# Dilated-window attention and a leaky-ReLU MLP in one kernel: joined value casts in the first two batches, two entries of the planner's cost list, and another order of the first loads

## The chip, the cores and the metric

The kernel runs on one core of one Trainium2 chip. The metric is the device time of one launch in microseconds (us). The kernel before has a median of 294.21 us over 3 runs (293.82 to 296.23).

## The reference

Eight batches of 8 heads with 576 tokens and 64 features go through causal window attention. Heads 0 to 3 look back over 32 neighbouring tokens, heads 4 to 7 over 128 tokens in steps of 4 ("dilated"). The result is laid out as 4608 tokens by 512 features and goes through two matrix products with a leaky ReLU between them.

```
mask_plain = (rel >= 0) & (rel < window)
mask_dil = (rel >= 0) & (rel < window * dilation) & (rel % dilation == 0)
masks = np.stack([mask_plain if h < H // 2 else mask_dil for h in range(H)], axis=0)
scores = np.where(masks[None, :, :, :], scores, -1000000000.0)
attn = np.exp(scores - np.max(scores, axis=-1, keepdims=True))
attn = attn / (np.sum(attn, axis=-1, keepdims=True) + 1e-09)
x = np.matmul(attn, v).transpose(0, 2, 1, 3).reshape(B * S, H * D)
h = x @ w_in
return np.maximum(0.01 * h, h) @ w_out
```

Here window is 32, dilation 4, w_in is 512 x 2048 and w_out 2048 x 512. Inputs and output are float32; the kernel computes with float16 operands.

## The kernel before, in words

**Pairs of heads.** Two heads share a tile of 128 partitions. The program calls such a pair `vi`: pairs 0 and 1 are plain, 2 and 3 dilated, and they are visited in the order 2, 3, 0, 1. For each pair a region of the tile `slots` holds the keys and queries (features on partitions) and the values (tokens on partitions), all in float16.

**Two ways of doing attention.** Batches 0 and 1 (`EARLY`, line 29) are done before the rest of the kernel is under way. q and k arrive as float32 tiles `stg`, are cast to `nat` (line 701 when ACT casts, line 702 otherwise), turned by TensorE (line 940) into PSUM, and moved from there to `slots` (line 713 on ACT, 714 on DVE). A unit (line 1027 on) is half a pair: scores (lines 1073 and 1076), the exponential on ACT (1083), the sums (1094), the values product (1088), logarithm and exponential of the sums on ACT (1104 and 1106), and the product with the reciprocal into `xt` on DVE (1117). The last 64 tokens of all pairs are one more unit, "rest" (lines 1154 to 1193). Batches 2 to 7 are done in bursts on quarters of the array (line 1278) between other work.

**Value casts.** `load_v` (from line 765) fetches v for four heads at a time into `vst`: group 1 (`g == 1`, dilated) first, group 0 after it. In batches 0 and 1 the dilated group is cast to `slots` in 12 pieces, six for each of the two pairs: four of 64 partitions x 256 elements and two of 64 x 64. A pair's values product waits for the pair's own six.

**The MLP.** Chunks of 384 tokens run through `up` (line 1407, 16 blocks of 128 hidden features; in the first chunk each of the four `vi` blocks is a task by itself) or, for the second chunk, `up_pair` (line 1441), ACT evicts with leaky ReLU (1423, 1454), and the second product follows (line 1620 for the first tiles, 1709 after). From chunk 8 on the first product is done with seven instead of eight products (line 1540).

**What sets the order.** Nothing is issued in the order of the Python code. Every operation is added to a plan with the engines that may do it, a cost for each, and a priority. A list scheduler goes forward and backward over the plan (line 543 on), takes the backward times as priorities, adds a number per task from the table `NUDGE` (line 42), and lets the table `HAND` (line 282) cut a task's choice of engines. Its last forward pass fixes engine and order of every instruction. Idle stretches of TensorE in the plan are filled with matmuls on a tile of zeros, `warm` (line 1983), which keep it active and give nothing to the output. The costs of a cast stand in `cast` (line 695), those of a move out of PSUM in `move` (line 712 on).

**The first loads.** The string `FIRST` (line 40) is the order of the loads of batches 0 and 1 and of the weights: `q01` is q and k of batch 0, group 1, `r0` the last 64 tokens' q and k of batch 0, `v01` its dilated values, `w0` to `w7` the eight blocks of w_in (512 KB each; `w0` to `w3` are the first 1024 hidden features for pairs 2, 3, 0, 1), `w8` to `w15` those of w_out, `c` a table of constants. All go to SP's queue but k of `q01` and the constants with the identity matrix, which go to ACT's. Group 0's first q goes into `stg2`, and so on in turn.

## Time and profile before

| | |
|---|---|
| median of 3 runs | 294.21 us |
| the three runs | 296.23, 294.21, 293.82 us |
| the profiled execution's own time | 294.69 us |
| its span (first to last instruction) | 292.9 us |
| mean granted TensorE clock in it | 0.992 |
| PE busy, share of the span | 283.5 us, 97% |
| DVE, ACT, POOL busy | 225.0, 214.4, 87.8 us |
| real work of PE, without the matmuls on zeros | begins at 6.90 us with line 940 |
| first matmul of the MLP | 23.06 us |

How to read it: the page has busy time per engine, then the span in 40 slices with the busy share in tenths, the clock that the throttle granted to TensorE and the DMA share, then the chain of work that ended last, then groups of instructions. A table by stage shows the same for stretches of one's choice. A timeline row has start, length, engine, line, what is written and read, how many instructions are merged in the row, and in brackets how long the engine sat idle before it and what ended that.

### The profile page before, as it was taken

To read this page: it belongs to the slowest core of one execution; us is meant where nothing else is said; L and a number is where in the kernel's file an instruction comes from. 1 tells how busy PE (TensorE), PEld (TensorE's weight loads), DVE (VectorE), ACT (ScalarE), POOL (GpSimd) and SP (SyncE) were. 2 spreads that over 40 slices of the span, in tenths; PEclk is the share of its full clock that TensorE was granted. 3 is DMA by queue.
4 is the path that set the end of the run, shared out by engine and by line. 5 is a ranking of instruction groups with operands and counts; after the bars stand their busy time and mean duration, and the time that the engine had idled before them with its cause. 6 is when DMAs were issued, how large, how long until landed. Compare 5 with 4: busy or idle time off the path is not lost.

```text
span 292.9 us, 9624 instructions
## 1 busy us (share of the span) xinstructions
PE 283.5 (97%) x3983; PEld 222.1 (76%) x3983; DVE 225.0 (77%) x445; ACT 214.4 (73%) x451; POOL 87.8 (30%) x149
## 2 busy tenths in 40 slices
PE   7879999999999999999999999999999999999995
PEld 3656877686676767776767777878899999999984
DVE  6695577855789469965967978999987879888773
ACT  3996898688988996899888778895556777745421
POOL 4334532371371734352742752630200000000000
PEclk9979999999999999999999999999999999999999
DMA  7999999895999988799999888411212010112123
GB/s 253 316 350 402 388 289 325 225 229 83 143 188 198 214 153 168 138 200 226 180 206 176 163 171 199 134 40 38 73 38 74 1 38 2 36 38 74 47 98 107
DMA packets 140043, 47.04 MB, mean 161 GB/s; under 512 B 118752, under 2 KB 137440, under 8 KB 140000
## 3 DMA queue, kind: packets, MB, share of 16 engines
q1 hardware_dynamic: 139312, 45.81, 62.9%
q8 instruction: 31, 0.51, 0.7%
q10 hardware_dynamic: 688, 0.63, 0.6%
q14 instruction: 12, 0.10, 0.1%
HBM read 36.99 MB, written 9.44 MB: 158 GB/s over the span
## 4 chain that ended last, share of the span: by engine, by line
PE 88%; ACT 4%; DVE 3%; DMA 2%; issue 1%; ACTq 0%; DVEq 0%
PE psum L1709 32%; PE psum L1407 24%; PE psum L1540 13%; PE psum L1278 6%; PE psum L1620 5%; PE psum L1441 3%; DMA con<-consts 2%; PE psum L940 1%; DVE slots L702 1%; ACT slots L713 1%; PE psum L1094 1%; PE psum L1088 1%; DVE xt L1117 1%; PE psum L1073 1%; DVE slots L714 1%
## 5 line engine op out<-in xcount | busy, mean ns | idle before, releaser
L1407 PE MATMUL psum<-xt,w_in 128*128 128x384 f16 x448 | 84.8, 326 | 0.1
L1709 PEld LDWEIGHTS <-gt 128*128 128x128 f16 x768 | 74.5, 98 | 11.7 <-issue 0.5
L1423 ACT ACTIVATE gt<-psum 128x384 f16<-128x384 f32 x112 | 53.3, 492 | 15.0 <-PE psum L1407 13.0
L1709 PE MATMUL psum<-w_out,gt 128*128 128x256 f16 x512 | 63.6, 273 | 0.3 <-DVE stg L1740 0.3
L1407 PEld LDWEIGHTS <-w_in 128*128 128x128 f16 x448 | 41.7, 98 | 23.5 <-issue 0.5
L702 POOL CAST nat<-stg 128x576 f16<-128x576 f32 (+1 forms) x50 | 33.5, 693 | 43.5 <-DVE gt L1695 21.3
L702 POOL CAST slots<-vst 64x256 f16<-64x256 f32 (+4 forms) x56 | 27.0, 496 | 24.9 <-DMA vst<-in_v_dram 13.9
L1360 DVE TENSOR_TENSOR xt<-psum,rc 128x448 f16<-128x448 f32 (+2 forms) x52 | 20.3, 429 | 15.9 <-ACT rc L1343 14.8
L1559 DVE TENSOR_TENSOR vst<-psum,vst 128x384 f32<-128x384 f32 x48 | 25.7, 552 | 5.7 <-PE psum L1540 2.7
L1563 ACT ACTIVATE gt<-vst 128x384 f16<-128x384 f32 (+1 forms) x32 | 21.7, 684 | 7.9 <-DVE vst L1559 7.8
L701 ACT CAST slots<-vst 64x256 f16<-64x256 f32 (+4 forms) x54 | 22.5, 429 | 1.0
L1377 ACT ACTIVATE ee<-psum 128x896 f16<-128x896 f32 (+3 forms) x30 | 21.4, 721 | 2.5 <-PE psum L1278 2.4
L1552 ACT COPY vst<-psum 128x384 f32<-128x384 f32 x29 | 13.6, 475 | 11.7 <-PE psum L1540 11.2
L1540 PEld LDWEIGHTS <-w_in 128*128 128x128 f16 x256 | 21.9, 98 | 0.3
L1540 PE MATMUL psum<-xt,w_in 128*128 128x192 f16 x192 | 20.9, 246 | 0.0
L714 DVE COPY slots<-psum 128x512 f16<-128x512 f16 (+3 forms) x22 | 10.3, 477 | 11.5 <-PE psum L940 4.3
L1384 DVE TENSOR_TENSOR ee<-ee,con 128x768 f16<-128x768 f16 (+1 forms) x24 | 14.4, 599 | 6.2 <-ACT ee L1377 6.1
L1746 DVE TENSOR_TENSOR osb<-psum,stg 128x512 f32<-128x512 f32 x21 | 14.3, 682 | 4.1 <-ACT stg L1738 2.3
L926 POOL COPY slots<-slots 128x512 f16<-128x512 f16 (+1 forms) x15 | 10.2, 690 | 23.7 <-DVE slots L919 17.2
L1540 PEld LDWEIGHTS <-stg 128*128 128x128 f16 x192 | 16.7, 98 | 0.5
L1738 ACT COPY stg<-psum 128x512 f32<-128x512 f32 (+1 forms) x18 | 9.9, 549 | 9.6 <-PE psum L1709 9.0
L1343 ACT ACTIVATE rc<-rc 128x576 f32<-128x576 f32 x24 | 16.6, 691 | 0.1
(107 smaller groups left out, 501.7 us busy)
## 6 DMA issues: line engine op xcount, KB each, us to landing
out_dram<-osb SPq DMA_DIRECT2D x32, 256.0 KB, 2.6
stg<-in_q_dram SPq DMA_DIRECT2D x40, 144.0 KB, 3.5
stg<-in_k_dram SPq DMA_DIRECT2D x40, 144.0 KB, 3.7
vst<-in_v_dram SPq DMA_DIRECT2D x16, 288.0 KB, 4.8
vst<-in_v_dram SPq DMA_DIRECT2D x8, 512.0 KB, 5.9
gt<-in_moe_w_in_dram SPq DMA_DIRECT2D x6, 512.0 KB, 7.4
stg<-in_q_dram SPq DMA_DIRECT2D x5, 512.0 KB, 5.6
stg<-in_k_dram SPq DMA_DIRECT2D x5, 512.0 KB, 6.5
```

What stands on the lines that cost most here:

```text
L701: return nc.scalar.copy(out=dst, in_=src)
L702: return ENG[e].tensor_copy(out=dst, in_=src)
L1278: jobs.append(lambda: nc.tensor.matmul(at(bk, q0, q1, x, *od), lhs(p0, p1, q), rhs(p0, p1), start=first, stop=last, skip_group_check=True, ...
L1343: lambda e: nc.scalar.activation(out=rt, in_=rt, func=AF.Exp, scale=-1.0), prio)
L1360: lambda e, args=args: nc.vector.tensor_tensor(out=args[0], in0=args[1], in1=args[2], op=ALU.mult), prio)
L1377: lambda e, p=p, np=np, part=part: nc.scalar.activation(out=at(et, 0, 128, 448 * p, [448, np], [1, n]), in_=part, func=AF.Exp, scale=SCALE ...
L1407: nc.tensor.matmul(ht[:, 0:n], at(w_in, 0, 128, vi * DFF + j // 2 * 256 + j % 2, [2, 128]), at(xt[m % 2], 0, 128, vi * 1152 + x0 + x, [1, n]),
L1423: lambda e: nc.scalar.activation(out=gt[c % NG][:, j * n_c + x:j * n_c + x + n], in_=ht[:, 0:n], func=AF.Prelu, alpha=0.01),
L1540: nc.tensor.matmul(bk[:, n * i:n * i + n], w(v, 2 * z + i), x(v), start=first and i == 0 and v == 0, stop=i == 1 and v == 1, skip_group_ch ...
L1559: return add("DVE", 0.08 + 2 * n * 0.00104, deps, lambda e: nc.vector.tensor_tensor(out=dst, in0=over(bk), in1=dst, op=ALU.add), begin + w ...
L1563: t = add("ACT", dur, deps + gt_free.get(c - NG, []), lambda e: nc.scalar.activation(out=dst, in_=src, func=AF.Prelu, alpha=0.01), begin + ...
L1709: nc.tensor.matmul(bk[:, x:x + HN], tl[:, off + j * step:off + j * step + 128], rhs(j), start=first and x == 0 and j == 0, stop=j == HJ - ...
```

## The change

It has five parts.

1. **Joined value casts.** In batches 0 and 1 the dilated group's casts take both pairs in one instruction: 64 x 2x4x64 and 64 x 2x64 in place of two of half the size. That makes 6 casts of 12 in each of the two batches. Both pairs' values products now wait for all six.
2. **Costs of casts.** DVE's listed cost gets a fixed part of 0.16 in place of 0.08, ACT's 0.20 in place of 0.085; the part per element stays.
3. **Cost of the dilated key moves.** Their listed cost per element on DVE goes from 0.00127 to 0.00052.
4. **The first loads.** `r0` comes before `q00`; `w3` comes before `w6`; some of the later ones change places.
5. **The tables.** `NUDGE` and `HAND` are replaced, `PLACE`, `PACE`, `SERVE` and the banks of the early turns (`TURN_AT`) are set a little differently.

Each PE matmul that computes something is there as often as before. Of those on zeros there are 3 more. Over the whole program DVE has 9 instructions more (456), ACT 13 fewer (443), POOL 8 fewer (146).

```diff
-SERVE = 1.1
+SERVE = 1.08
...
-PLACE = 20.5
-PACE = 4.6
+PLACE = 20.0
+PACE = 4.65
...
+OWN = 0.16
+JOIN = (0, 1)
...
-FIRST = ('q01 q00 r0 w7 v01 v00 w0 w1 w2 w6 w3 w4 q11 w5 w9 q10 v11 w10 '
-         'w8 w13 w11 r1 v10 w15 w12 w14 c ')
+FIRST = ('q01 r0 q00 w7 v01 v00 w0 w1 w2 w3 w6 w4 q11 w5 w9 q10 v11 w10 '
+         'w13 w8 w15 w11 r1 v10 w12 c w14 ')
 NUDGE = {
-    0: 87.72, 2: -74.14, 3: 109.34, 4: -121.33, 5: -62.38, 6: 44.63, 7: 83.91, 8: -101.47, 9: 29.63,
...
 HAND = {
-    3: "DVE", 4: "DVE", 5: "DVE", 6: "DVE", 8: "DVE", 11: "DVE", 12: "DVE", 13: "DVE", 26: "DVE",
...
+    9: "POOL", 26: "POOL DVE", 28: "ACT", 29: "POOL", 33: "DVE", 36: "DVE ACT", 45: "ACT", 48:
...
-TURN_AT = ('fgfgt', 't0tft')
+TURN_AT = ('1g1gt', 's0tft')
...
-                t.choices = tuple(c for c in t.choices if c[0] == HAND[t.n])
+                t.choices = tuple(c for c in t.choices if c[0] in HAND[t.n])
...
-        cost = {"POOL": (0.08 + n * 0.00108) * slow, "DVE": 0.08 + n * 0.00052,
-                "ACT": (0.085 + n * 0.00084) * slow}
+        cost = {"POOL": (0.08 + n * 0.00108) * slow, "DVE": OWN + n * 0.00052, "ACT": 0.04 + OWN + n * 0.00084}
...
-        for j in range(2):
+        for j in range(1 if b < EARLY and JOIN[g] else 2):
             vi = 2 * g + j
             tn, (users, old) = slot_of[b, vi], slot_users[b, vi]
-            made = []
+            made, twice, near = [], [], []
+            if b < EARLY and JOIN[g]:
+                old = old + slot_users[b, vi + 1][1]
+                twice, near = [[TS, 2]], [[512 if g else S, 2]]
...
-                made.append(cast(slot(tn, x, 64 * h, 64 * h + 64, *xd), at(vs, 64 * ab, 64 * ab + 64, y, *yd), n,
-                                 [lv[i]] + old, prio, SHIFT if h != ab else ("POOL",) if b >= EARLY else
-                                 ("POOL", "DVE", "ACT")))
+                if twice and n == 64:
+                    near = [[128, 2]]
+                made.append(cast(slot(tn, x, 64 * h, 64 * h + 64, *twice, *xd),
+                                 at(vs, 64 * ab, 64 * ab + 64, y, *near, *yd), n * (2 if twice else 1),
+                                 (lv if twice and not g else [lv[i]]) + old, prio,
+                                 SHIFT if h != ab else ("POOL",) if b >= EARLY else ("POOL", "DVE", "ACT")))
             v_in[b, vi] = made
+            if twice:
+                v_in[b, vi + 1] = made
...
-                               ("DVE", "ACT"), None, bank_k))
+                               ("DVE", "ACT"), True, bank_k))
```

Three places show how instructions move. In each, the rows of before stand first and those of the change after them. `L686` and `L642` are the same line of code, as are `L701` and `L656`, `L702` and `L657`, `L713` and `L668`, `L714` and `L669`.

The first is DVE between the first turned tile of batch 0 and the dilated value casts. `nat` and `rest` are q and k before they are turned, a copy of 128x4x128 is a dilated pair's queries, 64x8x64 are keys, 128x512 a plain pair's queries, 64x2x64, 128x2x64 and 128x2x4x16 belong to the rest, `vst_73` holds the dilated values.

```order
L714 COPY slots<-psum 128x4x128 x2
L714 COPY slots<-psum 64x8x64
L714 COPY slots<-psum 128x512
L702 CAST nat_72<-stg_67 128x2x4x64
L702 CAST rest<-stg_68 128x256
L702 CAST w_in<-wst_89 128x512
L714 COPY slots<-psum 64x2x64
L714 COPY slots<-psum 128x2x64
L702 CAST slots<-vst_73 64x4x64 x5
L702 CAST slots<-vst_73 64x64
```

```order
L669 COPY slots<-psum 128x4x128
L669 COPY slots<-psum 64x8x64 x2
L657 CAST rest<-stg_66 128x256
L657 CAST nat_71<-stg_67 128x2x4x64
L657 CAST nat_72<-stg_67 128x2x4x64
L669 COPY slots<-psum 128x2x64
L669 COPY slots<-psum 64x2x64
L669 COPY slots<-psum 128x512
L657 CAST w_in<-wst_89 128x512
L657 CAST slots<-vst_73 64x2x4x64 x2
L657 CAST slots<-vst_73 64x2x64
L657 CAST slots<-vst_73 64x2x4x64
```

Rows that repeat are left out in both: before has two copies of 128x512 and two of 64x8x64 there; the change has two of 128x512, three of 64x2x64, and four of 64x8x64, all four dilated key moves. DVE takes the dilated keys and one more cast of `nat`, and casts the dilated values in four instructions instead of six.

The second is ACT in the same stretch, from its two first casts to the casts of `vst_73`. `ee` is the exponential of scores, `rc` the sums.

```order
L713 COPY slots<-psum 64x8x64 x2
L701 CAST nat_71<-stg_66 128x2x4x64
L1083 ACTIVATE ee<-psum 128x320 x2
L713 COPY slots<-psum 64x8x64
L1104 ACTIVATE rc<-psum 128x256 x2
L1106 ACTIVATE rc<-rc 128x256 x2
L713 COPY slots<-psum 64x2x64
L1104 ACTIVATE rc<-psum 128x256
L701 CAST slots<-vst_73 64x4x64 x2
L1106 ACTIVATE rc<-rc 128x256
L701 CAST slots<-vst_73 64x64 x2
```

```order
L668 COPY slots<-psum 128x4x128
L1046 ACTIVATE ee<-psum 128x320 x2
L668 COPY slots<-psum 128x2x4x16
L1067 ACTIVATE rc<-psum 128x256
L668 COPY slots<-psum 64x2x64
L1069 ACTIVATE rc<-rc 128x256
L1046 ACTIVATE ee<-psum 128x320
L656 CAST nat_72<-stg_68 128x2x4x64
L668 COPY slots<-psum 64x8x64 x2
L656 CAST slots<-vst_73 64x2x4x64
```

ACT no longer begins with key moves. It has one joined value cast where it had four small ones, and it stands behind the three key moves of the plain pairs.

The third is PE just ahead of the first matmuls of the MLP (lines 1407 and 1370). `L1073` and `L1036`, `L1076` and `L1039`, `L1094` and `L1057` are the same lines; rows in between are left out.

```order
L1094 MATMUL psum<-ee,con 128x32
L1983 LDWEIGHTS warm
L1983 MATMUL psum<-warm 128x256
...
L1076 MATMUL psum<-slots 128x64
L1983 LDWEIGHTS warm
L1983 MATMUL psum<-warm 128x512
...
L1407 LDWEIGHTS w_in
L1407 MATMUL psum<-xt_79,w_in 128x384
```

```order
L1039 MATMUL psum<-slots 128x32
L1946 LDWEIGHTS warm
L1946 MATMUL psum<-warm 128x512
...
L1370 LDWEIGHTS w_in
L1370 MATMUL psum<-xt_79,w_in 128x384
...
L1057 MATMUL psum<-ee,con 128x192
```

A matmul of 128x32 on `slots` ends the scores of the last pair's first unit, one of 128x64 those of its second, the last of all. Before, the first MLP matmuls stand behind both, behind one matmul of 256 columns on zeros and four of 512. After the change four of 512 and the first three of the MLP stand directly behind the first unit's scores, and the sums, values and last scores follow them.

More of the change, by code (lines that the diff above doesn't have):

```diff
@@ L390, in forward @@
     def forward(self):
-        free, waiting, landed, ends = {}, {}, [], []
+        free, landed, ends = {}, [], []
+        waiting = {e: set() for e in ("PE", "ACT", "DVE", "POOL", "SP")}
         server = 0.0
```

37 lines of the change are left out of this document (10 added, 27 removed), and 447 rows, old and new, of the table NUDGE.

## The prediction

> **What bounds the kernel now.** I read the page first, then the table by stage, then the timeline of each engine up to 30 us.
>
> ```profile
> span 292.9 us, 9624 instructions
> PE 283.5 (97%) x3983; PEld 222.1 (76%) x3983; DVE 225.0 (77%) x445; ACT 214.4 (73%) x451; POOL 87.8 (30%) x149
> PE   7879999999999999999999999999999999999995
> PEclk9979999999999999999999999999999999999999
> PE 88%; ACT 4%; DVE 3%; DMA 2%; issue 1%; ACTq 0%; DVEq 0%
> ```
>
> PE is the bound: 97% of the span, 88% of the chain that ended last. Both dips in its row of digits are at the ends. The change removes no matmul that computes something, so it can only move the time at which PE becomes full, the few holes after that, and the clock. The table by stage says where those are.
>
> ```profile
> 12.00:16.00 4.00, 2.76 (x24) 1.47 (x23) 3.11 (x9) 3.82 (x12) 1.43 (x4) 1.00 1.11 275
> 16.00:20.00 4.00, 2.73 (x36) 2.02 (x37) 3.80 (x12) 3.76 (x11) 1.26 (x3) 0.85 1.00 356
> 40.00:50.00 10.00, 9.50 (x110) 6.93 (x108) 7.95 (x20) 8.60 (x25) 2.79 (x6) 1.00 0.98 299
> 50.00:60.00 10.00, 9.68 (x120) 7.15 (x119) 8.53 (x17) 6.70 (x20) 3.77 (x5) 1.00 0.88 246
> 280.00:293.00 13.00, 9.79 (x90) 8.52 (x88) 6.57 (x14) 1.86 (x5) 0.00 (x0) 0.96 0.29 102
> ```
>
> The columns are stretch, length, busy time of PE, PEld, DVE, ACT and POOL, then the granted clock, DMA share and GB/s. After 40 us the holes are 0.50 and 0.32 us, and 3.2 us at the end, where the last results are moved out; the change does not touch that end. Ahead of 20 us PE is full for less than 70% of the time, and ACT is the fullest engine there (3.82 and 3.76 of 4.00). So the stage to look at is the attention of batch 0.
>
> ```profile
> 13.93 1.35 PE L1983 MATMUL psum<-warm 128*128 128x512 f16 x6
> 16.33 0.63 PE L1088 MATMUL psum<-ee,slots 128*128 128x96 f16 x8 [1.05 <-DVE slots L702]
> 17.93 0.30 PE L1088 MATMUL psum<-ee,slots 128*128 128x96 f16 x4 [0.75 <-DVE xt L1117]
> 20.74 0.37 PE L1983 MATMUL psum<-warm 128*128 128x256 f16 x1
> 22.17 1.05 PE L1983 MATMUL psum<-warm 128*128 128x512 f16 x4
> 23.06 0.65 PE L1407 MATMUL psum<-xt,w_in 128*128 128x384 f16 x3
> ```
>
> PE waits 1.05 us for the dilated value casts on DVE and 0.75 us for the bank that DVE's product frees, and from 20.74 us on it spends 1.42 us on zeros (0.37 + 1.05). With the first MLP matmul at 23.06 us it is full.
>
> **The change part by part.** I sum against the profiled execution, 294.69 us (its span of 292.9 us and 1.8 us around it); it lies 0.5 us over the median of 294.21 us, and I carry the difference over to the median.
>
> *Joined value casts.* What one costs is not in the trace; its neighbours are.
>
> ```profile
> L702 DVE CAST slots<-vst x11: 176/291/540, 14.4 to 19.8; 64x256 f16<-64x256 f32 x7, 64x320 f16<-64x320 f32 x3, 64x64 f16<-64x64 f32 x1
> L701 ACT CAST slots<-vst 64x256 f16<-64x256 f32 x9 | 3.6, 402 | 0.2
> L701 ACT CAST nat<-stg 128x512 f16<-128x512 f32 x3 | 1.9, 618 | 1.2 <-DMA stg<-in_k_dram 0.8 <-DMA stg<-in_q_dram 0.4
> 12.91 0.43 DVE L702 CAST w_in<-wst 128x512 f16<-128x512 f32 x1
> 14.44 1.85 DVE L702 CAST slots<-vst 64x256 f16<-64x256 f32 x6
> ```
>
> On DVE a joined cast of 512 elements lies between one of the halves and two of them, 0.29 and 0.58 us; 512 elements in another shape take 0.43 us, which I take. On ACT it lies between 0.40 and 0.80 us; I take 0.62 us. So a pair of casts saves about 0.15 us of DVE or 0.18 us of ACT, 12 pairs some 2 us of engine time. None of it is on PE's path by itself. What counts is when the first values product may start, which is when the casts end. Before, DVE reached its six at 14.44 us and ended at 16.29. The first row below is of the table by stage, the others are of the timeline.
>
> ```profile
> 7.54:14.44 6.90, 5.71 (x72) 4.24 (x71) 4.80 (x12) 6.67 (x18) 2.69 (x6) 1.00 1.14 317
> 7.54 0.42 DVE L714 COPY slots<-psum 128x512 f16<-128x512 f16 x1 [1.55 <-PE psum L940]
> 9.09 0.43 DVE L714 COPY slots<-psum 64x512 f16<-64x512 f16 x1 [0.22 <-PE psum L940]
> 9.81 0.69 DVE L714 COPY slots<-psum 128x512 f16<-128x512 f16 x1 [0.30 <-PE psum L940]
> 11.59 0.28 DVE L702 CAST rest<-stg 128x256 f16<-128x256 f32 x1
> 13.94 0.48 DVE L714 COPY slots<-psum 64x128 f16<-64x128 f16 x2 [0.61 <-ACT slots L713]
> 13.54 0.57 POOL L702 CAST slots<-vst 64x256 f16<-64x256 f32 x2 [1.10 <-DMA vst<-in_v_dram]
> ```
>
> By the new order DVE has ahead of them, from the same first move on: dilated queries 0.42, four dilated key moves 4 x 0.43, the rest's cast 0.28, three casts of 512 elements 3 x 0.43, two plain queries 2 x 0.69, and four small moves 4 x 0.25 (0.48 us for two). That is 6.1 us, so it comes to the values at 13.6 us if it never waits. Before, it was busy 4.8 of the 6.9 us from 7.54 to 14.44, so it waited 2.1; with the same waits it comes there at 15.7 us. The values themselves land at 13.5 us (POOL's cast), and no load ahead of them is added or dropped. Three joined casts and a small one take 3 x 0.43 + 0.2 = 1.5 us. The first values product may then start between 15.1 and 17.2 us, against 16.33: a gain of 1.2 to a loss of 0.9 us. ACT's joined cast stands behind much of the softmax and may end last. I take no change, and note that the second pair, which began at 17.93 us, has its casts by then in any case and waits for the bank alone.
>
> *Moves and casts between engines.* Up to the eviction of the first MLP block ACT loses two moves of 64x512, a small move, four value casts of the dilated group and a cast of w_in; it gains a move of 128x512, a joined cast and a plain value cast.
>
> ```profile
> L713 ACT COPY slots<-psum 64x512 f16<-64x512 f16 x8 | 4.6, 578 | 2.0 <-PE psum L940 1.4 <-DVE slots L714 0.5
> L701 ACT CAST slots<-vst 64x64 f16<-64x64 f32 x3 | 0.7, 243 | 0.1
> L701 ACT CAST slots<-vst 64x320 f16<-64x320 f32 x1 | 0.5, 458 | 0.0
> L701 ACT CAST w_in<-gt 128x512 f16<-128x512 f32 x1 | 0.6, 607 | 0.0
> 25.14 0.39 ACT L1106 ACTIVATE rc<-rc 128x224 f32<-128x224 f32 x1
> ```
>
> Taking 0.58 for a 128x512 move too and 0.26 for a small one: 2 x 0.58 + 0.26 + 2 x 0.40 + 2 x 0.24 + 0.61 = 3.3 us off, 0.58 + 0.62 + 0.46 = 1.7 us on, so ACT has 1.6 us less. The last exponential of batch 0's units, at 25.14 us, can come that much earlier. It is worth little: from 23.06 us on PE has MLP blocks to do, and they hide it. Without that cover it would be worth all of 1.6 us. I put it at nothing beyond the next item.
>
> *The first MLP matmuls.* The new order puts four matmuls on zeros and then MLP work directly behind the scores of the last pair's first unit, which stood ahead of the row at 20.74 us. The 1.42 us on zeros become four matmuls of 512 columns: 0.9 us if the clock is full (five and a half such took 1.35 us at 13.93, the last one's tail among it), twice that if it is half. At full clock 0.5 to 0.6 us is gained, at half 0.3 lost; sooner readiness of ACT and DVE could take away all 1.42. I take a gain of 0.6 us, within -1.4 to +0.3.
>
> *Loads.* The rest's q and k go ahead of group 0's.
>
> ```profile
> 6.90 0.61 PE L940 MATMUL psum<-con,nat 128*128 128x128 f16 x8 [0.99 <-DMA con<-consts]
> 8.83 0.61 POOL L702 CAST nat<-stg 128x512 f16<-128x512 f32 x1 [0.80 <-DMA stg<-in_k_dram]
> 9.72 0.40 POOL L702 CAST rest<-stg 128x256 f16<-128x256 f32 x1 [0.27 <-DMA stg<-in_k_dram]
> ```
>
> The rest landed 0.9 us after group 0's k. Changed round, the plain pairs' k comes 0.9 us later, at 9.7 us, and the rest 1 to 3 us sooner. The first turn waits 0.99 us for the constants on ACT's queue; other loads beside them may shift that, by nothing to at most 0.99 us. Either shift ends at the wait for the values at 13.5 us, so the cost is nothing; with that cover gone it is up to 0.9 us either way. `w3` ahead of `w6` helps the fourth product of the first blocks, where PE was full.
>
> *Later holes.* The whole order after 30 us is another one. The holes of 0.50 and 0.32 us can vanish or as many and twice as long ones come: within -0.8 and +1.6 us. I take -0.4, half of them gone, since half of the 2 us of cast time comes off DVE and ACT there, for batch 1.
>
> *The clock.* The granted clock is full or half, in stretches of 3.41 us.
>
> ```profile
> 5.17:8.58 3.41, 1.95 (x17) 1.10 (x16) 1.38 (x4) 1.78 (x4) 1.26 (x2) 1.00 1.10 373
> 15.41:18.82 3.41, 1.71 (x26) 1.28 (x27) 3.29 (x10) 3.14 (x9) 1.28 (x3) 1.00 0.95 336
> 18.82:22.24 3.42, 3.26 (x37) 2.76 (x35) 2.84 (x7) 3.09 (x9) 1.00 (x2) 0.50 1.00 375
> 22.24:25.65 3.41, 3.41 (x51) 2.35 (x50) 0.88 (x3) 2.13 (x6) 1.17 (x2) 1.00 1.05 392
> ```
>
> It was half from 18.82 to 22.24 us, behind a stretch in which PE was busy 1.71 of 3.41 us; behind one with 1.95 it stayed full. Half of the 3.26 us that PE worked there, 1.6 us, is what it cost at most. The new order has as much zero work and the same waits around 16 us, so I leave it as it is. The Trainium skill's page "TensorE: Matmul & The Clock Gate" (Part 1, "What's actually happening") has the clock fall to half after at least one idle window of about 3.4 us. This trace differs: it fell behind a window in which PE was half busy. By the page's rule the fall would not be there, before or after, and the sum would stay as it is.
>
> **Sum.** 0 (casts) + 0 (ACT) - 0.6 (first MLP matmuls) + 0 (loads) - 0.4 (later holes) + 0 (clock) = -1.0 us. That is 293.7 us for the profiled execution and 293.2 us for the median.
>
> **The rivals.**
>
> *The clock stays full* (A). If the new order keeps PE busier than 1.71 us ahead of its full stretch, the 1.6 us go too, and 293.2 becomes 291.6 us; with the larger gain ahead of the MLP (1.4 in place of 0.6) it is 290.8. For it: 1.71 and 1.95 us lie close, and 0.24 us of PE work more is enough. Against: the waits of 1.05 and 0.75 us have no sure reason to go. The page named above also says, in the same part, that the window runs freely and is not tied to the start of the kernel. By that the stretches would lie elsewhere in other executions, and part of the 2.4 us between the runs shown would come from it.
>
> *The joined cast on ACT comes last* (B, slower). A pair's first values product now waits for both pairs' casts. ACT has its joined cast behind the softmax of the dilated pairs and three plain key moves of 0.58 us. If those moves wait for keys that come 0.9 us later, and the cast's own 0.62 us comes on top, the values start 1.5 us later than 16.33, PE stands for as long, and the emptier stretch halves the clock for a second 3.41 us, 1.6 us more: 294.2 + 3.1 = 297.3 us; without the second, 295.7. It decides from the point where ACT's cast ends later than DVE's three, which end between 15.1 and 17.2 us. Against: ACT had 1.6 us of work taken off, and most of that ahead of this cast.
>
> *It is hidden anyway* (C). The loads set the pace to 20 us, batch 0 ends where it did, and the new order keeps holes like the old one's: 294.2 us. For it: w_in's blocks come at the rate of the DMA, whose share is 0.95 and more in the rows from 12 to 26 us.
>
> **How the numbers follow.** The forecast has a chance of 0.46, A 0.24, B 0.15, C 0.15. About 1% is what a measurement of this kernel can tell from no change: 2.9 us, so 291.3 and 297.1 are the bounds. Faster by over 1%: half of A, with its larger gain, and a sixth of the forecast, where more of the holes go: 0.2. Slower by over 1%: half of B and a little of the rest for holes that are not foreseen, 0.1. Within 1%: 0.7. The range reaches down to A with a part of its larger gain, 290.8, and up to B without the second half clock and 0.2 us of new holes, 295.9.
>
> **What would show it.** In the profile after: first MLP matmul between 21 and 22.5 us instead of 23.06; PE's wait ahead of the first values product about 1 us as before, and released by DVE or ACT casts; the second values product sooner behind the first than 1.6 us; a joined DVE cast of 0.4 to 0.45 us and ACT's near 0.62; one half clock stretch. Holes between 40 and 60 us should sum to about 0.4 us. The prediction is wrong if the first MLP matmul is earlier than 21 us or later than 23.5, if the granted clock has no or two half stretches, or if PE has holes of over 1 us behind 30 us.

## The result and the profile after

The changed kernel takes 291.67 us (median of 4, 291.57 to 291.85), the kernel before beside it 294.89 us (median of 4, 293.82 to 296.23). The ratio is 0.9893, with a 95% interval from 0.9854 to 0.9932. In a later series it was 0.9893 again (0.9867 to 0.9920). The change gains 3.2 us between the medians, about 1%. Of the executions in the sections below, two (296.74 us of after_loads_back and 327.14 us of after_mlp_late, granted clock 0.852) lie over 1.5% above the fastest of their kernel and are left out of every comparison.

Lines of the changed kernel lie 37 lower from the turns on (1407 is now 1370, 1088 is 1051) and 45 lower at the casts and moves (701 and 702 are 656 and 657, 713 and 714 are 668 and 669). First some lines of its page: busy time, the span in 40 slices, and shares of the chain that ended last.

```profile
span 289.8 us, 9625 instructions
PE 281.3 (97%) x3986; PEld 220.9 (76%) x3986; DVE 228.2 (79%) x454; ACT 213.7 (74%) x438; POOL 83.0 (29%) x141
PE   8789999999999999999999999999999999999995
PEclk9999999999999999999999999999999999999999
PE 91%; ACT 3%; DMA 2%; DVE 1%; issue 1%; SPq 1%; DVEq 0%
```

The profiled execution takes 291.57 us, 3.1 less than that of before, and its span is 3.1 us shorter. PE is still the bound. The third slice of the clock, which had a 7 before, has a 9. The table by stage shows where PE became fuller (stretch, length, busy time of PE, PEld, DVE, ACT and POOL, granted clock, DMA share, GB/s).

```profile
12.00:16.00 4.00, 3.19 (x31) 1.87 (x31) 3.82 (x11) 3.19 (x7) 0.74 (x2) 1.00 1.08 258
16.00:20.00 4.00, 3.24 (x44) 2.12 (x45) 3.71 (x11) 3.94 (x11) 0.61 (x1) 1.00 0.94 339
40.00:50.00 10.00, 10.00 (x121) 7.44 (x120) 7.70 (x22) 8.71 (x25) 2.25 (x4) 1.00 0.89 276
50.00:60.00 10.00, 10.00 (x140) 7.45 (x138) 9.79 (x23) 7.11 (x16) 5.23 (x7) 1.00 1.10 312
```

From 12 to 20 us PE is busy for 6.43 us in place of 5.49, and between 40 and 60 us no hole is left. The first of these is not more work that computes. The table by stage for the matmuls on zeros alone, before and after (here busy time of PE, PEld and POOL), shows it:

```profile
12.00:20.00 8.00, 1.73 (x7) 0.61 (x7) 0.00 (x0) 0.93 1.06 316
12.00:20.00 8.00, 3.62 (x15) 1.23 (x15) 0.00 (x0) 1.00 1.01 298
```

Zeros take 3.62 us there in place of 1.73, so some 2.8 us are left for what computes, in place of 3.8. PE is fuller there because more of its waits hold zeros.

The timeline of PE around the first values products and the first MLP matmuls:

```profile
12.05 0.61 PE L903 MATMUL psum<-con,nat 128*128 128x128 f16 x8 [1.02 <-DVE slots L669]
14.66 0.92 PE L1946 MATMUL psum<-warm 128*128 128x512 f16 x4
15.94 0.46 PE L1051 MATMUL psum<-ee,slots 128*128 128x96 f16 x8 [0.36 <-ACT slots L656]
17.49 0.45 PE L1051 MATMUL psum<-ee,slots 128*128 128x96 f16 x8
19.30 1.02 PE L1946 MATMUL psum<-warm 128*128 128x512 f16 x4
20.16 0.65 PE L1370 MATMUL psum<-xt,w_in 128*128 128x384 f16 x3
```

The values products come at 15.94 and 17.49 us (before 16.33 and 17.93). The first MLP matmul comes at 20.16 us, 2.9 us sooner than before. PE's longest wait in this part is now an earlier one, 1.02 us at 12.05. The dilated key moves, which now stand on DVE, have ended by then (at 9.42 us). What releases it is a move of a plain pair's queries, which stands on DVE behind two casts of `nat` and two small moves:

```profile
11.31 0.69 DVE L669 COPY slots<-psum 128x512 f16<-128x512 f16 x1
```

To see when a lead arises, I took from both traces the time by which PE has issued the same amount of work that computes (matmuls weighed by their columns, those on zeros left out). The two orders differ, so an entry holds to about 0.2 us, and ahead of 20 us, where they differ most, to about 0.5 us. The third column compares with a run of the kernel before with nothing but more zeros, whose clock stayed full (experiment 2).

| work of PE that the kernel before has done at | changed minus before | changed minus before at full clock |
|---|---|---|
| 9.0 us | -0.8 | -1.0 |
| 12.0 us | +0.3 | +0.1 |
| 19.2 us | -0.3 | -0.9 |
| 23.7 us | -1.9 | -1.3 |
| 37.2 us | -2.1 | -1.3 |
| 48.0 us | -2.2 | -1.2 |
| 60.0 us | -2.7 | -1.7 |
| 101.6 us | -2.9 | -1.9 |
| 108.5 us to the end | -3.4 | -2.4 |

So the lead at full clock is made in three places: ahead of 24 us, between 48 and 60 us, and between 101 and 108 us. Some 0.3 us is lost again in the tail, where the last results are moved out (spans 289.8 and 291.9 us at full clock, -2.1).

### The profile page after: what moved, and what is told of

Read it like the earlier page. It is cut to its first block, busy times and chain, and to the rows that moved or that the text cites. A ratio compares the mean times of both kernels' runs of the same rounds, so it can differ in the third digit from the quotient of the medians.

```text
span 289.8 us, 9625 instructions
## 1 busy us (share of the span) xinstructions
PE 281.3 (97%) x3986; PEld 220.9 (76%) x3986; DVE 228.2 (79%) x454; ACT 213.7 (74%) x438; POOL 83.0 (29%) x141
## 4 chain that ended last, share of the span: by engine, by line
PE 91%; ACT 3%; DMA 2%; DVE 1%; issue 1%; SPq 1%; DVEq 0%
PE psum L1672 34%; PE psum L1370 25%; PE psum L1503 13%; PE psum L1241 6%; PE psum L1583 5%; PE psum L1404 3%; DMA stg<-in_k_dram 2%; PE psum L903 1%; ACT slots L668 1%; ACT slots L656 1%; DVE slots L669 1%; PE psum L1039 1%; PE psum L1036 1%; PE psum L1051 1%; ACT gt L1386 1%; PE psum L1057 1%
## 5 line engine op out<-in xcount | busy, mean ns | idle before, releaser
L657 POOL CAST nat<-stg 128x576 f16<-128x576 f32 (+1 forms) x45 | 32.1, 731 | 59.8 <-DVE ee L1347 21.0
L657 POOL CAST slots<-vst 64x256 f16<-64x256 f32 (+4 forms) x54 | 25.1, 477 | 21.7 <-DVE gt L1658 10.0
L1347 DVE TENSOR_TENSOR ee<-ee,con 128x768 f16<-128x768 f16 (+1 forms) x24 | 15.5, 647 | 11.0 <-ACT ee L1340 10.9
L1701 ACT COPY stg<-psum 128x512 f32<-128x512 f32 (+1 forms) x22 | 11.8, 537 | 15.2 <-PE psum L1672 11.1
L656 ACT CAST slots<-vst 64x448 f16<-64x448 f32 (+4 forms) x47 | 21.3, 462 | 0.9
L1515 ACT COPY vst<-psum 128x384 f32<-128x384 f32 x31 | 14.6, 474 | 5.4 <-PE psum L1503 5.1
L669 DVE COPY slots<-psum 128x512 f16<-128x512 f16 (+3 forms) x33 | 13.5, 431 | 5.8 <-PE psum L903 5.0
L1299 ACT ACTIVATE rc<-psum 128x576 f32<-128x576 f32 x24 | 15.6, 649 | 2.9 <-PE psum L1241 2.0
L882 DVE STREAM_TRANSPOSE slots<-nat 128x576 f16<-128x576 f16 (+2 forms) x30 | 15.7, 555 | 1.1 <-POOL nat L657 1.1
```

The lines of the kernel that those rows point to most:

```text
L656: return nc.scalar.copy(out=dst, in_=src)
L657: return ENG[e].tensor_copy(out=dst, in_=src)
```

## The experiments

Each edit below is made in the finished order, so that everything not named keeps its engine and its place. Each execution comes with its mean granted clock, which says how many stretches of 3.41 us ran at half clock: 0.998 to 1.000 none, 0.992 to 0.994 one, 0.988 two. The table sorts the executions by that.

The executions were taken in four series. The kernel before has medians at full clock of 293.95, 294.01, 293.74 and 294.02 us in them, so a difference between kernels of two series holds to about 0.3 us.

| kernel | none: n, median us | one | two | ratio to before, 95% interval |
|---|---|---|---|---|
| before, beside the others | 35: 293.95 | 41: 294.91 | 10: 296.04 | 1 |
| changed, two series | 10: 291.68 | 0 | 0 | 0.9893 (0.9867 to 0.9920) |
| after_fewer_zeros | 5: 291.55 | 6: 293.19 | 1: 293.96 | 0.9925 (0.9901 to 0.9949) |
| before_more_zeros | 8: 294.05 | 4: 295.30 | 0 | 0.9993 (0.9969 to 1.0016) |
| after_split_casts | 7: 292.06 | 0 | 0 | 0.9914 (0.9880 to 0.9947) |
| after_loads_back | 8: 292.41 | 3: 293.54 | 0 | 0.9936 (0.9910 to 0.9962) |
| before_rest_first | 4: 293.23 | 8: 293.98 | 0 | 0.9968 (0.9951 to 0.9985) |
| after_mlp_late | 5: 292.22 | 0 | 0 | 0.9911 (0.9891 to 0.9932) |
| before_mlp_early | 5: 294.36 | 7: 295.42 | 0 | 1.0003 (0.9986 to 1.0021) |
| before_holes | 6: 295.07 | 5: 296.05 | 1: 296.84 | 1.0029 (1.0008 to 1.0049) |
| before_three | 12: 293.00 | 0 | 0 | 0.9948 (0.9924 to 0.9972) |
| after_tuned | 6: 292.02 | 0 | 0 | 0.9907 (0.9871 to 0.9943) |
| after_held0 | 5: 291.18 | 0 | 0 | 0.9882 (0.9856 to 0.9907) |

### 1. Zeros taken out of the changed kernel (after_fewer_zeros)

```diff
 L1057 MATMUL psum<-ee,con 128x2x64
-L1946 MATMUL psum<-warm 128x512
-L1946 MATMUL psum<-warm 128x512
-L1946 MATMUL psum<-warm 128x512
-L1946 MATMUL psum<-warm 128x256
 L1051 MATMUL psum<-ee,slots 128x96
...
-L1946 MATMUL psum<-warm 128x512
-L1946 MATMUL psum<-warm 128x512
...
-L1946 MATMUL psum<-warm 128x512
```

> The changed kernel without seven of the matmuls on zeros between 14.6 and 18.1 us (all between the exponential sums of the third unit and the scores of the last pair but one); nothing that is computed changes. If the clock is set by how busy PE is in a window, the window from 15.5 to 18.9 us falls from 2.29 to about 1.35 us busy, the next one is granted half, and the kernel takes up to 1.7 us longer: about 293.3 us, against 291.7. If the full clock of the changed kernel has another cause (the window's phase, the loads), or if the zeros cost time themselves, it stays at 291.7 us or gains a few tenths, with no half stretch.

Of 12 executions 7 had half stretches, against 0 of 10 of the changed kernel. At full clock it takes 291.55 us, which cannot be told from the changed kernel's 291.68; with one half stretch it takes 1.6 us more. The profiled execution has one. The table by stage, cut at its own windows:

```profile
15.46:18.87 3.41, 1.12 (x20) 0.92 (x21) 3.02 (x9) 3.33 (x9) 0.45 (x1) 1.00 0.96 310
18.87:22.28 3.41, 3.41 (x24) 2.04 (x24) 1.89 (x6) 1.80 (x5) 1.28 (x2) 0.50 0.97 370
```

PE is busy 1.12 us of one window, and the next is granted half. The zeros cost nothing there that can be told and hold the clock in this order: the first theory stands. They are no guarantee in another one, since after_loads_back (experiment 4) has all of them and a half stretch in 3 of 11 executions.

### 2. Zeros added to the kernel before (before_more_zeros)

```diff
 L1983 MATMUL psum<-warm 128x256
+L1983 MATMUL psum<-warm 128x512
+L1983 MATMUL psum<-warm 128x512
+L1983 MATMUL psum<-warm 128x512
+L1983 MATMUL psum<-warm 128x512
 L1088 MATMUL psum<-ee,slots 128x96
...
 L1076 MATMUL psum<-slots 128x64
+L1983 MATMUL psum<-warm 128x512
+L1983 MATMUL psum<-warm 128x512
+L1983 MATMUL psum<-warm 128x512
```

> The kernel before with seven more matmuls on zeros of 512 columns: four in PE's wait of 1.05 us ahead of the first values product, three in its wait of 0.75 us ahead of the second pair's. If the clock is set by how busy PE is, the window from 15.41 to 18.82 us goes from 1.71 to about 3.3 us busy, the half stretch from 18.82 to 22.24 us is gone, and the kernel gains up to 1.6 us: about 293.2 us against 294.9. If the half clock only covered waits that remain (for exponentials and for blocks of w_in), the clock is full and the time stays at 294.5 us or more. If the clock falls only behind an empty window, the half stretch stays and so does the time.

The profiled execution has no half stretch, but by the times this is a miss: the ratio cannot be told from 1. Two things were unforeseen. The kernel before has no half stretch in 35 of its 86 executions anyway, so the edit could only improve the others (4 of 12 kept one, none had two). And a half stretch costs the kernel before 1.0 us between the medians (0.7 to 1.6 us in the single series), not 1.6. Three of the seven zeros also came behind the second wait, not into it.

The order of the kernel before up to 38 us is the same in experiment 7, and there the clock stayed full without any added zero. The table by stage of that kernel (before_holes), cut at its own windows:

```profile
14.03:17.44 3.41, 2.32 (x22) 1.28 (x22) 2.94 (x11) 3.24 (x10) 0.66 (x2) 1.00 0.92 288
17.44:20.85 3.41, 2.33 (x39) 1.77 (x37) 3.25 (x9) 3.24 (x10) 1.23 (x2) 1.00 0.93 320
```

They lie 1.4 us ahead of those of the kernel before, whose rows the prediction shows. There one window (15.41 to 18.82 us) holds both waits and has 1.71 us of work; here the waits are divided between two windows with 2.32 and 2.33 us, and the clock stays full. This fits a clock that is decided by where the windows lie in an execution, with the kernel only setting how little work a window can hold. But the same trace has a window that does not fit a bound in PE's busy time:

```profile
3.79:7.20 3.41, 1.44 (x7) 0.59 (x6) 2.00 (x5) 1.24 (x2) 0.66 (x1) 1.00 1.08 375
```

It holds less busy time than the 1.71 us behind which the clock fell, and the next window (7.20 to 10.62 us) is granted in full. The last section comes back to this.

### 3. The join undone (after_split_casts)

```diff
         def fn(e):
-            if e == "ACT":
-                return nc.scalar.copy(out=dst, in_=src)
-            return ENG[e].tensor_copy(out=dst, in_=src)
+            for to, of in halves or ((dst, src),):
+                if e == "ACT":
+                    made = nc.scalar.copy(out=to, in_=of)
+                else:
+                    made = ENG[e].tensor_copy(out=to, in_=of)
+            return made
```

> The changed kernel with each joined value cast made as two casts again, one behind the other on the same engine, everything else in its place: 12 more casts for batches 0 and 1. If the join itself matters, DVE's seven casts from 13.59 us take some 0.6 us longer (3 x 0.15 for those of 512 elements and two smaller), ACT's 0.18 us, and the first products of the second pair wait as long: 0.3 to 0.6 us slower, 292.0 to 292.3 us. If the join is worth nothing by itself, as the prediction put it, and all of the gain is from the order: 291.7 us within 0.2, and the first values product at 15.9 us within 0.2.

At full clock the median is 292.06 us against 291.68, with ranges that overlap (291.52 to 294.58, and 291.30 to 293.04), so by time alone it is not settled. In the trace the changed kernel's lead over it is 0.2 us by 24 us and 0.5 us from 42 to 58 us, the difference made at the second batch's casts. Behind 96 us this profiled execution, the slowest of the seven (294.58 us), loses 2.7 us more; the other six are at least 1.8 us shorter, so that loss says nothing of the join. The timeline of PE at the second batch's casts, first this kernel, then the same two groups of matmuls in the changed one (`L1042` is `L1036`):

```profile
39.12 0.30 PE L1042 MATMUL psum<-con 128*128 128x192 f16 x2 [0.52 <-DVE slots L672]
40.38 0.30 PE L1042 MATMUL psum<-con 128*128 128x192 f16 x2
```

```profile
38.19 0.30 PE L1036 MATMUL psum<-con 128*128 128x192 f16 x2
39.84 0.30 PE L1036 MATMUL psum<-con 128*128 128x192 f16 x2 [0.16 <-DVE xt L1080]
```

With the join undone PE waits 0.52 us ahead of the first group, for a DVE move that now stands behind two casts in place of one; the changed kernel waits 0.16 us ahead of the second. A second execution of the changed kernel (after_again) waits 0.38 us there, so 0.2 us of the 0.5 lies within what one and the same program shows. The join is worth 0.2 to 0.5 us by the traces, mostly in batch 1.

### 4. The first loads, undone and alone (after_loads_back, before_rest_first)

```diff
 L642 DMA stg_64<-in_q_dram 128x2x256 x2
+L642 DMA stg_67<-in_q_dram 128x4x256
+L642 DMA stg_68<-in_k_dram 128x4x256
 L642 DMA stg_66<-in_q_dram 64x8x64
 L642 DMA stg_66<-in_k_dram 64x8x64
-L642 DMA stg_67<-in_q_dram 128x4x256
-L642 DMA stg_68<-in_k_dram 128x4x256
```

> The changed kernel with the plain pairs' q and k loaded ahead of the rest's again, as in the kernel before; the rest of the order stays. If the earlier constants (6.00 against 6.86 us) come from this exchange, the first turn goes back from 6.05 to about 6.9 us. If that shift ends at the later waits, as the prediction put it, the time stays at 291.7 us within 0.3; if it carries through to the MLP it is about 292.5 us. The casts of the rest stand early on DVE, so DVE waits up to 1 us longer for them ahead of the dilated moves.

The second run makes the opposite exchange in the kernel before:

```diff
+L686 DMA stg_68<-in_q_dram 64x8x64
+L686 DMA stg_68<-in_k_dram 64x8x64
...
-L686 DMA stg_68<-in_q_dram 64x8x64
-L686 DMA stg_68<-in_k_dram 64x8x64
```

> The kernel before with the rest's q and k loaded ahead of the plain pairs', as in the changed kernel; nothing else. If this exchange alone brings the constants in earlier, they land at about 6.0 us in place of 6.86 and the first turn is at 6.05 us. If that is worth what undoing it cost the changed kernel (0.7 us at full clock), the time is about 293.2 us at full clock against 293.95. If the gain ends at later waits, as the prediction put it, or at the plain pairs' k that now comes 0.9 us later in an order that was made for the other loads, 294 us or somewhat more.

Undone, it costs 0.73 us at full clock (292.41, from 292.18 to 293.91, against 291.68); done alone, it gains 0.78 us (293.23 against 294.01 of the kernel before beside it). PE's first turn, changed kernel with the loads back, then the kernel before with the rest first:

```profile
7.39 0.61 PE L903 MATMUL psum<-con,nat 128*128 128x128 f16 x8 [1.44 <-DMA con<-consts]
16.95 0.46 PE L1051 MATMUL psum<-ee,slots 128*128 128x96 f16 x8 [0.36 <-ACT slots L656]
21.17 0.65 PE L1370 MATMUL psum<-xt,w_in 128*128 128x384 f16 x3
```

```profile
6.06 0.61 PE L940 MATMUL psum<-con,nat 128*128 128x128 f16 x8 [0.60 <-DMA con<-consts]
```

Undoing the exchange moves the first turn of the changed kernel from 6.05 to 7.39 us; making it moves that of the kernel before from 6.90 to 6.06 us. In both, the later turn waits for the constants, which land later when the larger loads go first. All profiled executions agree: the first turn lies between 6.03 and 6.46 us in the nine with the rest's loads first and between 6.90 and 7.43 us in the five with the plain pairs' first. In the changed kernel the sequence then follows: of the 1.34 us, 1.01 us are left at the first values product and still at the first MLP matmul, and 0.9 us at the end of this trace. Only a third is absorbed.

### 5. The first MLP matmuls, put back and put forward (after_mlp_late, before_mlp_early)

```diff
 L1039 MATMUL psum<-slots 128x32
-L1946 MATMUL psum<-warm 128x512 x4
-L1370 MATMUL psum<-xt_79,w_in 128x384 x3
...
-L1370 MATMUL psum<-xt_79,w_in 128x384
...
 L1039 MATMUL psum<-slots 128x64
+L1946 MATMUL psum<-warm 128x512 x4
+L1370 MATMUL psum<-xt_79,w_in 128x384 x4
```

> The changed kernel with its four matmuls on zeros and the first four MLP matmuls put behind the scores of the last unit, where the kernel before has them. If the place matters, PE stands for exponentials at 19.3 us with nothing to do, the first MLP matmul comes at 21.5 us or later in place of 20.16, and the kernel loses 0.6 to 1.3 us: 292.3 to 293.0 us. If the exponentials and w_in set the pace there anyway, 291.7 us within 0.3. The zeros that now stand later leave the wait empty, so a half clock stretch may come in some executions; those at full clock are to be compared.

It loses 0.54 us (292.22 us). PE's timeline shows which wait the MLP work had covered:

```profile
19.91 0.30 PE L1057 MATMUL psum<-ee,con 128*128 128x192 f16 x3 [0.38 <-ACT ee L1046]
20.98 1.03 PE L1946 MATMUL psum<-warm 128*128 128x512 f16 x4
21.84 1.30 PE L1370 MATMUL psum<-xt,w_in 128*128 128x384 f16 x7
```

The opposite edit in the kernel before, with the cast of w_in that gates it put from ACT to POOL:

```diff
 L1076 MATMUL psum<-slots 128x32
+L1983 MATMUL psum<-warm 128x512 x4
+L1407 MATMUL psum<-xt_79,w_in 128x384 x3
...
-L1983 MATMUL psum<-warm 128x256
...
-L1983 MATMUL psum<-warm 128x512 x4
-L1407 MATMUL psum<-xt_79,w_in 128x384 x3
...
-L701 CAST w_in<-gt_82 128x512
...
-L702 CAST w_in<-gt_82 128x512 x3
+L702 CAST w_in<-gt_82 128x512 x4
```

> The kernel before with four matmuls on zeros and the first three MLP matmuls put ahead of the last unit, where the changed kernel has them; so that they can start there, one cast of w_in goes from ACT (21.91 us) to POOL behind its neighbour, and one matmul on zeros of 256 columns goes. If the place of the first MLP work is what the changed kernel gained at full clock by 23 us (1.3 us), the first MLP matmul comes at 20.2 to 20.8 us and the kernel gains 0.6 to 1.3 us: 292.7 to 293.4 us at full clock, against 293.95. If PE only waits behind it instead (for exponentials and for w_in), 293.95 us within 0.3.

It gains nothing (294.36 us at full clock against 294.01). Its first MLP matmul comes at 21.06 us, but PE then waits 0.28 us for a logarithm further on. So the place was worth 0.5 us in the changed order and nothing in the old one; which part of the changed order it needs was not tried.

### 6. The matmuls on zeros ahead of the MLP (after_held0, after_tuned, after_again)

```diff
-HELD = 4
+HELD = 0
```

> The changed kernel without the four matmuls on zeros ahead of its first MLP matmul (19.30 to 20.16 us), nothing else. In the run before this one, which had two further exchanges that gave nothing, PE did its work 0.8 us sooner by 20 us and kept that up to 36 us. If that lead holds to the end, about 290.9 us, 0.8 us less than the changed kernel beside it. If the loads decide by the execution (that run's times lay between 290.97 and 292.69 us at full clock), no difference that can be measured: 291.5 to 292 us.

> The changed kernel itself once more, beside the version without its four matmuls on zeros, and for the share of its executions at full clock. If its matmuls on zeros hold the clock, as the runs without seven of them say, most or all executions show no half stretch and the median is 291.7 us within 0.4; the kernel before, beside it, has half stretches in half of its executions or more.

Side by side the two have medians of 291.18 us (291.08 to 291.72, 5 executions) and 291.77 us (291.30 to 293.04, 6 executions). PE's timeline without the zeros:

```profile
19.28 0.65 PE L1370 MATMUL psum<-xt,w_in 128*128 128x384 f16 x3
19.81 0.30 PE L1057 MATMUL psum<-ee,con 128*128 128x192 f16 x3
36.88 0.65 PE L1370 MATMUL psum<-xt,w_in 128*128 128x384 f16 x3 [0.37 <-ACT gt L1386]
```

The MLP starts 0.88 us sooner and no wait takes the zeros' place; in the trace the lead over the changed kernel is at least 0.8 us up to 36 us and 0.5 us at the end. It is the best version here, though 0.6 us between so few executions is at the edge of what can be told. No execution of it had a half stretch.

The version after_tuned had two exchanges besides, at the holes at 37.71 and 39.84 us (an eviction ahead of a value cast on ACT, a product ahead of a cast on DVE):

```diff
-L656 CAST slots<-vst_73 64x2x4x64
 L1386 ACTIVATE gt_81<-psum 128x384
+L656 CAST slots<-vst_73 64x2x4x64
...
-L657 CAST w_out<-gt_83 128x512
 L1080 TENSOR_TENSOR xt_79<-psum,rc 128x128x2
+L657 CAST w_out<-gt_83 128x512
```

> The changed kernel carried on: no matmuls on zeros ahead of the first MLP matmul (four, 0.9 us at 19.30), the eviction that PE waits for at 37.71 us (0.37) ahead of a value cast on ACT, and the product that it waits for at 39.84 us (0.16) ahead of the second of two casts on DVE. If the zeros only fill a place that MLP work could have, and the holes are the order's, the first MLP matmul starts at 19.3 to 19.6 us and the kernel gains 0.5 to 1.0 us: 290.7 to 291.2 us. If PE then waits as long for the exponentials that end at 20.2 us, only the holes are gained, 0.2 to 0.4 us. If it falls below what keeps the clock, half stretches come and the median rises above 291.7 us.

The median is 292.02 us, and the times lie in two groups, 290.97 and 291.07 us and then 291.94 to 292.69 us, all at full clock. The exchange of the eviction and the cast moved the hole to the cast's reader:

```profile
36.79 0.65 PE L1370 MATMUL psum<-xt,w_in 128*128 128x384 f16 x3 [0.25 <-ACT gt L1386]
38.15 0.30 PE L1051 MATMUL psum<-ee,slots 128*128 128x96 f16 x4 [0.34 <-ACT slots L656]
```

The hole of 0.37 us became two of 0.25 and 0.34. That does not explain the median: the trace is that of the fastest execution (290.97 us), and by 101 us it is as far ahead as that of after_held0. What the slower four lost is in no trace and stays open.

### 7. The later holes of the kernel before (before_holes, before_three)

The kernel before waits at 51 us for exponentials that stand behind five small moves on ACT, and at 104 us for a chain that begins behind three value casts on ACT. The timeline of PE, ACT and DVE there:

```profile
51.62 0.34 PE L1094 MATMUL psum<-ee,con 128*128 128x160 f16 x2 [0.32 <-ACT ee L1083]
104.58 1.91 PE L1709 MATMUL psum<-w_out,gt 128*128 128x256 f16 x16 [0.27 <-DVE stg L1740]
49.78 1.24 ACT L713 COPY slots<-psum 128x128 f16<-128x128 f16 x5
99.19 1.60 ACT L701 CAST slots<-vst 64x448 f16<-64x448 f32 x3
102.46 0.62 DVE L1360 TENSOR_TENSOR xt<-psum,rc 128x448 f16<-128x448 f32 x1 [2.98 <-ACT rc L1343]
```

First I only changed the order on the same engines (DVE's exchange at 41 us is left out here):

```diff
+L1083 ACTIVATE ee<-psum 128x416
+L1083 ACTIVATE ee<-psum 128x320
 L713 COPY slots<-psum 64x2x64
...
+L1336 ACTIVATE rc<-psum 128x576
+L1423 ACTIVATE gt_81<-psum 128x384
+L1343 ACTIVATE rc<-rc 128x576
 L701 CAST slots<-vst_74 64x448 x3
```

> The kernel before with the work in front of its three later holes exchanged, on DVE and ACT alone: the two products that free the score bank (hole of 0.50 us at 41.64) ahead of a key move of 0.68 us; two exponentials (0.32 us at 51.62) ahead of four small moves; the logarithm and exponential of a sum (0.27 us at 104.58, behind 2.98 us in which DVE waited) ahead of three value casts. Nothing that is computed changes. If what the changed kernel gains behind 50 us (0.6 us at 51, 0.2 to 0.5 at 104) is such holes and a closed hole counts to the end, the kernel gains 0.9 to 1.1 us. If work that is put back makes new holes, or the end is set by something else, less than 0.4 us.

It is slower by 1.1 us at full clock (295.07 against 294.01). At 51 us the hole closed, which gave 0.5 us, and 0.3 us of it was given back by 57 us. The exchange at 41 us gave nothing. At 104 us the run of three casts now stands ahead of an eviction that PE needs (PE, then ACT):

```profile
103.15 1.46 PE L1407 MATMUL psum<-xt,w_in 128*128 128x384 f16 x8 [1.04 <-ACT gt L1423]
104.88 1.91 PE L1709 MATMUL psum<-w_out,gt 128*128 128x256 f16 x16 [0.26 <-DVE stg L1740]
101.11 1.60 ACT L701 CAST slots<-vst 64x448 f16<-64x448 f32 x3
```

The run costs in both places that were tried on ACT. So the next kernel moves the three casts to DVE, which idled 2.98 us there, and two of the five small moves at 49.78 us as well; it also has the zeros of experiment 2 and the loads of experiment 4.

```diff
-L701 CAST slots<-vst_74 64x448 x3
...
-L702 CAST slots<-vst_74 64x448
+L702 CAST slots<-vst_74 64x448 x4
```

> The kernel before with three edits together: the rest's q and k loaded first (alone worth 0.78 us at full clock); the seven matmuls on zeros ahead of the values products (worth nothing at full clock, but fewer half stretches); and two runs of short work taken apart that stand on ACT ahead of what PE waits for: two of the five small moves ahead of the exponentials of 51 us go to DVE, and the three value casts at 99.2 us go to DVE too, which idled for 2.98 us there. No computation changes. If runs on ACT made the holes at 51.6 and 104.6 us, the first closes by about 0.4 us and the second by 0.4 to 0.6 us, and the whole comes to 292.2 to 292.7 us at full clock, against 294.0 of the kernel before and 291.7 of the changed one. If they only go elsewhere, as the exchange of their order did, it stays at 293.2 us, what the loads alone give.

All 12 executions ran at full clock, with a median of 293.00 us. Beside it the kernel before takes 293.74 us at full clock, so the three edits together gain 0.74 us, no more than the loads did alone, and less than the 292.2 to 292.7 us that was expected. The trace separates the places. At 104 us the hole is closed and 0.5 us is gained to the end:

```profile
101.52 1.46 PE L1407 MATMUL psum<-xt,w_in 128*128 128x384 f16 x8
102.82 1.91 PE L1709 MATMUL psum<-w_out,gt 128*128 128x256 f16 x16
```

At 51 us it got worse by 0.2 us, because one of the moves left on ACT now waited for DVE's, with the exponentials behind it:

```profile
50.37 0.34 PE L1094 MATMUL psum<-ee,con 128*128 128x160 f16 x2 [0.55 <-ACT ee L1083]
49.51 0.26 ACT L713 COPY slots<-psum 64x128 f16<-64x128 f16 x1 [0.67 <-DVE slots L714]
```

So the hole at 104 us is explained by the run of casts (by the trace; the times are too close to tell); that at 51 us is only located. Both tries to close it made a new wait, and what makes the changed order free of it (there most of these moves stand singly or in twos on DVE, with ACT's exponentials between) was not tried by itself.

## Why the prediction was right and wrong

The measured 291.67 us lies in the range (290.8 to 295.9) and 1.5 us below the forecast. By the prediction's own signs it was wrong twice: the first MLP matmul came ahead of 21 us, and the granted clock had no half stretch. Term by term:

**Joined casts, 0.** The durations were right. By shape, with 64x512 the joined ones:

```profile
L656 ACT CAST slots<-vst 64x512 f16<-64x512 f32 x3 | 1.9, 618 | 0.1
L657 DVE CAST slots<-vst 64x512 f16<-64x512 f32 x3 | 1.3, 434 | 0.1
```

They are 0.62 and 0.43 us, as taken. The first values product at 15.94 us lies between 15.1 and 17.2, and ACT's joined cast released it. The wait ahead of it was 0.36 us, not 1 us, and the second product followed after 1.55 us in place of 1.60, hardly sooner. That the join gives nothing was a little too low: it gives 0.2 to 0.5 us in the trace of experiment 3, not settled by the times. The text looked at batch 0 and left out batch 1.

**ACT's relief, 0.** Not tested by itself. What it was to be hidden by, MLP work, does cover PE in the profile after.

**First MLP matmuls, -0.6.** The direction was right, the mechanism was not. The prediction took its gain from zeros shortened from 1.42 to 0.9 us. The four zeros do take 0.86 us (19.30 to 20.16), but the 1.42 us count the matmuls' tails too. Up to the next matmul's start they were 0.23 (20.74 to 20.97) and 0.89 us (22.17 to 23.06), 1.12 us together, so the shortening is 0.26 us. By experiment 6 the four that are left are waste as well. The gain that was missed is that MLP matmuls now cover waits for exponentials (0.5 us, experiment 5).

**Loads, 0.** This step failed. It held that a shift at the start "ends at the wait for the values at 13.5 us". The prediction's own rows speak against it: the values landed at 13.5 us, but DVE came to them only at 14.44. They were not the last to come in the changed kernel either, where DVE begins on them at 13.59 us: the joined cast on ACT stood at the end of a sequence of moves, exponentials and casts that begins at the first turn, and most of a shift there goes through it (1.01 of 1.34 us). Measured in place of nothing: 0.73 us when undone, 0.78 us alone.

**Later holes, -0.4.** Sized too small: in the traces -0.5 between 48 and 60 us and -0.5 between 101 and 108 us. The prediction gave 0.50 and 0.32 us as all the holes between 40 us and the end and missed one of 0.27 us at 104.58, where a chain of ACT and DVE waits ended in a hole. The run of three casts on ACT accounts for that one.

**The clock, 0.** Wrong for the profiled execution, which lost 0.8 us to it by 37 us before (the table above: -1.3 against -2.1) and nothing after. The step that failed is "as much zero work and the same waits around 16 us": from 12 to 20 us the zeros take 3.62 us in place of 1.73, and the wait ahead of the first values product is 0.36 us in place of 1.05. Experiment 1 shows that without seven of these zeros the half stretches come back. Rival A's condition came true, PE is busier than 1.71 us in every window ahead of its full stretch:

```profile
8.69:12.11 3.42, 2.01 (x29) 1.55 (x26) 3.25 (x8) 3.02 (x11) 1.29 (x2) 1.00 1.06 351
12.11:15.52 3.41, 3.01 (x29) 1.75 (x28) 3.26 (x10) 2.74 (x6) 0.36 (x2) 1.00 1.18 278
15.52:18.93 3.41, 2.29 (x35) 1.54 (x35) 3.12 (x8) 3.33 (x9) 0.37 (x1) 1.00 0.88 318
18.93:22.34 3.41, 3.41 (x45) 2.40 (x43) 1.88 (x6) 2.58 (x9) 1.23 (x2) 1.00 0.97 374
```

But its price of 1.6 us was not right for the kernel before. There a half stretch costs 1.0 us (293.95 against 294.91); in the changed kernel without seven zeros it costs 1.6 us (291.55 against 293.19). That PE waits for part of that stretch anyway in the one and has MLP work all through it in the other would explain this; it was not tested. And 35 of 86 executions of the kernel before have none. So 291.6 us, which rival A gave, was met by another sum. At full clock the change gains 2.3 us (293.95 to 291.68); the clock adds 0.7 us on the medians of all executions (294.69 to 291.68 in all).

The Trainium skill's page "TensorE: Matmul & The Clock Gate" (Part 1, "What's actually happening") says that the window runs freely and does not start with the kernel. The runs agree: the first record of the full clock begins between 3.79 and 6.94 us in the profiled executions, and the half stretches lie whole windows behind that. The same section of the Trainium skill has the clock fall after at least one idle window. The traces differ: it fell behind windows in which PE was busy for 1.71, 1.57 and 1.12 us of 3.41.

**Rivals B and C.** B's place was right (ACT's joined cast does come last), its price was not: PE waits 0.36 us there, less than before. C is excluded by the time.

What the single terms measure, 0.75 (loads), 0.2 to 0.5 (join), 0.5 (place of the MLP), 0.5 (51 us, from the table alone) and 0.5 (104 us), sums to 2.5 to 2.8 us against 2.3 measured at full clock. They were taken in different orders and need not add, and 0.3 us is lost in the tail. That the measured time fell inside the range owes something to luck: the sum had the loads, the join and the clock at nothing, and it was their gains that brought the time to the lower end.

## What to carry to other kernels

Before saying that a shift at the start is absorbed by a later wait, follow what releases that wait back to the start: if it is an engine at the end of a sequence that begins with the shifted event, the shift goes through. A run of short instructions on an engine that also serves the critical one costs what it stands ahead of. Changing the order on the same engine moved the hole or made a new one in the places tried here (51 and 104 us of the kernel before, 37 us of the changed one). An engine that idled at that time took it away at 104 us; at 51 us, where the two engines then needed an order between them, it did not. Matmuls on zeros count as busy time, so a fuller PE in a table by stage need not be a PE that gets more done. Where a kernel leaves PE about half busy for a window, look at the clock of every execution, not at one profile.

## What the runs showed of the hardware

The clock falls behind windows of 3.41 us in which PE is partly busy, not only behind idle ones: behind 1.71, 1.57 and 1.12 us of busy PE it fell to half for one window, behind 1.79 (after_loads_back, 5.25 to 8.66 us), 1.95, 2.01 and 2.32 us it did not. In the kernel with the rest's loads first:

```profile
14.50:17.91 3.41, 1.57 (x18) 0.83 (x17) 3.26 (x11) 3.14 (x9) 0.58 (x1) 1.00 0.92 305
17.91:21.32 3.41, 3.41 (x41) 3.01 (x39) 2.75 (x7) 3.03 (x10) 1.54 (x3) 0.50 0.94 330
```

Two windows show that PE's busy time alone is not the measure. Behind the 1.44 us of before_holes (3.79 to 7.20 us, shown in experiment 2) and behind 1.59 us in the tail of after_held0 (284.28 to 287.70 us) the clock stayed full. So between 1.44 and 1.71 us both were seen. The window of 1.44 us holds 7 matmuls and those that fell hold 18 to 26, so what counts may be something other than the modelled busy time; that stays open. One and the same kernel has no, one or two half stretches, with medians of 293.95, 294.91 and 296.04 us, and this makes up much of its spread; the groups overlap (293.40 to 294.90 us and 294.27 to 296.22 us for the first two).

Single executions also carry stalls that belong to no kernel: the profiled execution of the changed kernel in the second series (293.04 us) lost 1.3 us between 163 and 190 us that the first profile, of the same program, does not have. What caused them stays open.
